# Attention and MLP on one core: the key corners written by a maximum or on ScalarE, the identity loaded first, and a new written order of all tasks

## The chip, the core and the metric

The kernel runs on one core of one Trainium2 chip. The metric is the device time of one execution in microseconds (us). The core has five engines that run side by side: TensorE (PE in the profile; its weight loads stand under PEld), VectorE (DVE), ScalarE (ACT), GpSimd (POOL) and SyncE (SP). Each engine works through its own list of instructions in order, and waits at an instruction whose inputs are not there yet. TensorE writes into PSUM, which has eight banks here, and transfers run on DMA queues that SP, ACT and POOL fill.

## What is computed

An attention with a relative bias over 8 batches, 8 heads, 576 positions and a head size of 64, followed by an MLP with a sine over all 4608 tokens:

```python
scores = scale * np.matmul(q, k.transpose(0, 1, 3, 2)) + bias      # bias depends on |i - j| alone
attn = np.exp(scores - max); attn = attn / (np.sum(attn) + 1e-09)
x = np.matmul(attn, v)                                              # heads side by side: 4608 x 512
h = x @ w_in                                                        # 512 -> 2048
s = np.sin(alpha * h)
g = h + s * s / (alpha + 1e-09)
return g @ w_out                                                    # 2048 -> 512
```

## The kernel before

The work is a graph of 1791 tasks (`_graph`, line 46). Each task has a key, the engines that it may run on, what it emits and what it depends on. The string `ORDER` (line 313) lists the keys in one sequence that was written in advance; `_planned` reads it, and each engine gets its instructions in exactly this sequence. A word is a key, with the PSUM bank behind a slash for TensorE's tasks, and with a letter there (A for ACT, D for DVE, G for POOL) where a task leaves its usual engine. Nothing is rescheduled at run time.

The keys that matter here, with t the batch 0 to 7, p the pair of heads 0 to 3, w the half of the queries and h the half of the keys:

- `n`, `t`, `c`: for t below 3, a load of q or k by POOL's queue (L550), its transposes on TensorE (L654, L670) and the copy out of PSUM by DVE or ACT (L619, L617). For t of 3 and more, `g` stages q or k in DRAM as fp16 on POOL's queue (L577) and `k` reads it back transposed on SP's queue (L583).
- `T`, `X`, `S`: the score tiles. `T` (L727) is four matmuls on 64 rows of the array each; `X` and `S` (L714, L687, L692) do the 64 positions that are left of 576 after four blocks of 128. `E` with the key behind it is the exponential on ACT (L734, L701), `B` with the key is the product with the bias on DVE (L755, L739, L742, L707).
- `o`: the key corners (L589). For t of 2 and more, the last 64 keys of a pair of heads are put on the diagonal of the tile `kd`, by two DVE copies of 64 partitions by 256 elements, SBUF to SBUF; `X` and `S` of the same t read `kd`.
- `A` and `N`: probabilities times v (L769, L778) and the division (L788, L789). `Y` brings the result transposed into `xT`, by SP's queue (L795) for t of 1 and more.
- `I`, `Z`, `Q`, `G`: the MLP's first product (L812), the sine on ACT (L818), its square on DVE (L825) or ACT (L823), and g on DVE (L830), for nine blocks of 512 tokens. `O`, `W`, `D` are the second product (L840), its eviction on DVE or ACT and the store.
- At the start: `r` are the four first loads of q and k, `f` their casts (L617, L619), `id` the load of the identity matrix that every transpose reads (L521), `j` the loads of the bias bands (`toep`, L628) and `m` the four masks that are cut out of them (two copies each, L634).

v is loaded by POOL's queue (`v` L556, `y` L562), as are the weights (L567, L572).

Of the kernel before, what the change touches and what calls it, by code (L numbers as in the profile page):

```python
# [318 lines left out]
EX00 n120 BT0111 X03/4 m0 ET0010 S0/7 BT0000 T0311/2 t101/6 BX00 ES0 BT0001 ET0311 c101 A000/7 m2
BX01 EX03 T0300/0 n131 BT0011 A010/6 BT0010 ET0300 BT0110 T0301/2 N000 m3 X02/4 N010 ET0301  # L320
T0201/0 n201 BS0 t100/7 BT0300 A011/6 v10 EX02 c100 y11 T0210/2 ET0201 BX03 T0310/4 N011 A001/7
n211 ET0210 BT0301 BT0311 n210 A030/6 ET0310 N001 v12 T0200/0 T1000/2 N030 t121/7 ET0200 n231
t111/5 BT0310 c121 t120/6 y10 t130/4 ET1000 T0211/0 BT0201 t131/7 c120 n200 ET0211 T1001/2 c111
A031/6 n230 ET1001 c130 wi3 t221/5 N031 T1110/0 c131/A v13 X10/2 c221/A BX02 T1111/6 BT0200 wi2
P03/4 EX10 BT0211 A020/5 wi1 ET1110 Y03 P01/3 BT0210 P00/2 A021/4 ET1111 N020 Y01 T1011/0 y20 N021
T1100/6 ET1011 t201/5 v11 t231/3 Y00 P02/4 c201 ET1100 X11/0 v23 Y02 S1/5 t200/2 c231 EX11 t210/4
wo0 T1101/6 BT1100 I0.14/3 ES1 wo2 ET1101 c210 wo1 T1010/0 BT1011 X12/4 ET1010 c200 I0.12/7 BT1001
EX12 BT1111 I0.1/6 v22 BX11 Z0.12 BS1 t230/2 BT1000 t211/5 I0.8/4 BT1010 c211 BX10 I0.3/1 Z0.14
BT1110 Q0.12 n220 Q0.14/A BT1101 I0.7/5 G0.12 v20 Z0.3 G0.14 I0.10/0 Z0.1 wo3 Q0.3 Z0.7 A110/7
Q0.1 g41 G0.3 Z0.8 I0.5/3 Q0.7/A G0.1 I0.13/1 c230/A G0.7 Q0.8/A I0.9/6 N110 v21 Z0.10 G0.8 I0.0/7  # L330
Z0.5 Q0.10 Z0.13 Q0.5 A100/2 G0.10 Q0.13/A I0.2/5 Z0.9 G0.5 y21 I0.4/4 Q0.9/A G0.13 Z0.2 N100
A101/3 Z0.4 G0.9 Z0.0 I0.6/2 Q0.4 g31 Q0.2/A G0.4 I0.11/6 Q0.0/A G0.2 Z0.6 I0.15/4 N101 Z0.11
T1300/0 Q0.6 Z0.15 A111/5 G0.0 ET1300 G0.6 O0.0/7 O0.2 Q0.11 Q0.15 T1210/2 O0.4 G0.15 O0.6 ET1210
G0.11 T1200/0 O0.8 BX12 ET1200 N111 T1201/2 t220/6 ET1201 T1211/4 Y11 c220 X13/0 O0.10 ET1211
BT1200 O0.12 o2 T1301/2 EX13 BT1211 T1310/4 O0.14 BT1201 ET1301 A120/6 W0 T1311/0 ET1310 BT1210 D0
X20/2 N120 O1.0/7 BT1301 ET1311 BT1300 S2/6 A121/5 Y10 BX13 EX20 O1.2 N121 T2001/0 ES2 T2011/2
BX20 ET2001 Y12 T2000/4 BT1311 O1.4 BT1310 A130/6 ET2000 O1.6 N130 ET2011 T2010/0 X22/4 A131/6
ET2010 T2211/2 EX22 N131 v31 T2100/0 O1.8 BT2010 Y13 ET2211 O1.10 BT2011 g40 O1.12 BT2000 O1.14
ET2100 BT2001 T2201/2 BS2 T2111/4 W1 ET2201 X21/0 v30 D1 A200/7 ET2111 BT2201 A201/6 g50 N200 EX21
T2210/2 N201 T2101/4 I1.1/7 ET2210 g30 T2110/0 ET2101 BT2210 T2200/2 BT2111 I1.13/6 ET2200 BT2100  # L340
I1.0/5 BT2101 BX22 ET2110 v32 BT2211 I1.4/4 BX21 Z1.13 BT2200 y31 I1.11/3 BT2110 y30 I1.6/2 v33
Z1.4 Q1.13 O2.0/1 Z1.0 G1.13 I1.3/0 Z1.1 Q1.4 O2.2 Q1.0 Q1.1/A I1.9/6 G1.4 Z1.11 G1.0 I1.12/4 Z1.3
G1.1 Q1.11/A I1.5/5 Q1.3 Z1.12 G1.11 I1.2/7 Z1.6 Q1.12 Q1.6/A G1.3 I1.14/3 Z1.5 G1.6 I1.15/0 Z1.2
G1.12 Q1.2/A I1.8/2 Q1.5 Z1.15 G1.2 I1.7/4 Z1.9 G1.5 Q1.9/A I1.10/7 Q1.15 Z1.7 G1.15 k30 A220/5
Q1.7/A G1.9 A221/0 Z1.8 N220 Z1.14 A210/6 G1.7 Z1.10 O2.4 N221 Q1.10/A T2311/4 k31 O2.6 Q1.8
ET2311 N210 A211/0 G1.10 O2.8 N211 O2.10 T2300/6 Q1.14 Y20 X23/4 G1.8 ET2300 O5.0/0 G1.14 O5.2
EX23 T2310/6 Y22 T2301/2 O2.12 ET2310 O2.14 T3000/4 ET2301 k40 T3001/6 BT2310 BT2300 O5.4 ET3001
O5.6 o3 O5.8 W2 O5.10 ET3000 BX23 T3010/2 BT2311 X30/6 ET3010 Y21 BT2301 S3/1 O5.12 BT3000 X31/4
ES3 EX30 O5.14 A230/1 W5 EX31 T3100/2 N230 T3110/6 D5 A231/0 ET3100 BT3001 BX31 D2 BS3 BX30
T3101/4 ET3110 v40 BT3100 T3211/2 A300/1 BT3010 ET3211 N231 g51 O4.0/7 O4.2 N300 Y23 ET3101 O3.0/6  # L350
BT3211 T3210/0 T3011/2 o4 T3111/4 ET3210 O4.4 g70 BT3101 O4.6 ET3011 O4.8 O4.10 ET3111 BT3011
T3201/0 X32/2 g61 ET3201 O4.12 A301/5 EX32 A310/4 N301 v41 T3200/0 X33/2 BT3201 Y30 N310 ET3200
I2.1/5 v42 BT3111 EX33 I2.10/4 BX32 y41 k41 Z2.1 y40 O4.14 I2.9/3 g60 I2.15/2 W4/A Q2.1 I2.5/1
Z2.10 BT3200 Z2.9 I2.14/7 Q2.10 G2.1 Q2.9/A A320/0 G2.10 Z2.14 I2.7/5 G2.9 Z2.15 Q2.15/A I2.3/4
N320 v43 Z2.7 Q2.14 I2.13/3 G2.15 Z2.3 G2.14 Q2.3/A I2.8/2 Z2.13 G2.3 I2.0/7 Z2.8 BT3210 Q2.7
I2.11/4 Q2.13/A G2.7 Q2.8/A I2.6/0 G2.13 Z2.11 G2.8 I2.4/5 Z2.5 Q2.11 Q2.5/A I2.2/3 G2.11 Z2.0
BT3110 O3.2 Z2.4 G2.5 I2.12/4 Z2.2 Q2.0 Q2.4/A G2.0 O3.4 S4/2 Q2.2/A O3.6 G2.4 A321/7 Z2.12 Z2.6
Q2.12 O3.8 BX33 ES4 A311/5 G2.2 Q2.6 O3.10 G2.6 O3.12 T3310/2 G2.12 T4001/0 O3.14 ET3310 N321
O7.0/4 ET4001 W3 O7.2 T3301/2 N311 T3311/6 O7.4 ET3301 Y31 O7.6 ET3311 T4000/0 T3300/2 O7.8 ET3300
D3 O6.0/5 O7.10 ET4000 k51 T4010/6 BT3300 X40/2 O6.2 ET4010 BT4000 O7.12 BT3310 T4100/0 EX40  # L360
BT4010 X41/6 BS4 BT4001 O6.4 BT3301 ET4100 BT3311 Y32 O6.6 A330/3 EX41 A331/2 N330 D4 T4011/0 N331
v53 T4210/6 O7.14 ET4011 BX40 O6.8 Y33 v51 W7 ET4210 T4101/2 T4211/0 BT4011 g71 O6.10 k50 ET4101
BT4100 A400/4 O6.12 ET4211 N400 T4111/2 T4200/6 BT4101 A401/4 BX41 y50 ET4111 v52 O6.14 ET4200
N401 T4201/0 y51 X42/2 W6 ET4201 I3.10/4 v50 BT4210 BT4211 EX42 T4110/6 BT4111 X43/0 A410/5 ET4110
I3.6/3 EX43 BT4110 BT4201 T4310/6 BX42 A411/2 BT4200 ET4310 N410 I3.3/1 Z3.6 I3.15/5 A420/0 Z3.3
Q3.6 I3.0/7 N411 Z3.10 I3.2/6 G3.6 Z3.0 Q3.3 Q3.0/A I3.12/2 G3.3 I3.1/3 N420 Z3.12 G3.0 Q3.10/A
I3.7/1 Z3.15 G3.10 I3.14/7 Q3.12/A Z3.2 I3.5/4 G3.12 Q3.15/A BX43 O8.0/0 Q3.2 Z3.7 A421/2 G3.15
Z3.14 G3.2 I3.8/5 Q3.7/A N421 Z3.5 I3.9/6 Z3.1 G3.7 Y42 I3.13/2 Q3.14/A o5 Z3.9 G3.14 I3.11/1 D7
Q3.5/A Y40 I3.4/7 Q3.9/A G3.5 Z3.13 Q3.1 O8.2 Z3.4 G3.9 O8.4 O9.0/4 Q3.13/A G3.1 O9.2 Q3.4/A G3.13
O8.6 Z3.8 O9.4 G3.4 O8.8 Z3.11 Q3.8 T4300/2 T4301/6 G3.8 O9.6 ET4300 BT4310 O8.10 Q3.11 O10.0/5  # L370
G3.11 O8.12 O8.14 ET4301 S5/1 O9.8 W8 O10.2 ES5 T4311/2 D8 T5001/6 T5000/0 ET4311 O10.4 k60 O9.10
ET5001 BT4311 O10.6 O9.12 BT4301 ET5000 BT4300 T5010/2 X50/6 ET5010 A430/1 BT5000 D6 O10.8 EX50
# [533 lines left out]
```

## Time and profile before

| | us |
|---|---|
| three runs | 389.81, 392.21, 392.63 |
| median of them | 392.21 |
| the profiled execution | 388.54 |
| its span, from first to last instruction | 386.6 |
| PE, ACT, DVE busy in the span | 371.4, 313.2, 271.3 |

The page shows one execution. Matmuls are pipelined, so a busy PE is not a PE that does useful work in every cycle; what it loses is better read from the times between the starts of its matmuls, and from the waits that the trace names. The clock that was granted to TensorE is 1.0 in every stage.

### The profile page before, as it was taken

What the parts mean: (1) busy time and instruction counts of PE and PEld (TensorE: products, weight loads), DVE (VectorE), ACT (ScalarE), POOL (GpSimd) and SP (SyncE); (2) the same over time, 40 slices, a digit from 0 to 9 for tenths busy, and PEclk for the clock granted to TensorE, in tenths of its full rate; (3) what the DMA queues carried; (4) which work ended last, traced back from release to release, by engine and by line L of the source; (5) the groups of instructions that cost most, each with busy time, mean ns of one, the idle gap of its engine ahead of it and who ended that gap; (6) DMA issues with size and microseconds to landing.
All of it is one profiled execution on the core that took longest, in us unless ns stands there. A gap on an engine that the chain in (4) does not pass through costs nothing.

```text
span 386.6 us, 9237 instructions
## 1 busy us (share of the span) xinstructions
PE 371.4 (96%) x3811; PEld 204.1 (53%) x3811; DVE 271.3 (70%) x625; ACT 313.2 (81%) x422; POOL 83.9 (22%) x100
## 2 busy tenths in 40 slices
PE   4999999999997999899999999999999999999996
PEld 3577455645554456554664544556555444444453
DVE  4599999679796977497668958685476577852311
ACT  5999999999996999899999999999895578654101
POOL 7878550470066004300000080000000000000000
PEclk9999999999999999999999999999999999999999
DMA  9999999999999969932938096031412011000115
GB/s 161 197 200 170 196 193 154 93 164 169 158 119 157 158 45 168 151 21 63 197 31 199 17 176 48 2 63 47 91 46 63 0 54 56 0 1 28 43 67 190
DMA packets 142617, 40.14 MB, mean 104 GB/s; under 512 B 127552, under 2 KB 138096, under 8 KB 142576
## 3 DMA queue, kind: packets, MB, share of 16 engines
q0 software_dynamic: 92672, 18.06, 57.0%
q1 hardware_dynamic: 47904, 18.94, 24.4%
q10 hardware_dynamic: 2000, 2.56, 1.9%
q8 instruction: 29, 0.48, 0.5%
q14 instruction: 12, 0.10, 0.1%
HBM read 36.89 MB, written 15.34 MB: 135 GB/s over the span
## 4 chain that ended last, share of the span: by engine, by line
PE 74%; DMA 9%; ACT 6%; DVE 5%; POOL 3%; issue 2%; SPq 0%; POOLq 0%; ACTq 0%
PE acc L840 29%; PE acc L812 26%; PE acc L778 7%; PE acc L727 6%; DMA w_in<-in_moe_w_in_dram 3%; ACT u L734 3%; DMA toep<-e_sb 2%; DMA xT<-xp 2%; PE acc L687 2%; PE acc L769 2%; ACT s L818 2%; DMA xT<-in_k_dram 2%; DVE g L830 1%; DVE kd L589 1%; POOL xT L550 1%
## 5 line engine op out<-in xcount | busy, mean ns | idle before, releaser
L734 ACT ACTIVATE u<-acc 128x1024 f16<-128x1024 f32 x160 | 152.0, 1035 | 13.4 <-PE acc L727 11.0
L840 PE MATMUL acc<-w_out,g 128*128 128x512 f16 (+1 forms) x592 | 141.8, 374 | 0.0
L812 PE MATMUL acc<-xT,w_in 128*128 128x512 f16 x576 | 135.0, 379 | 2.0 <-DMA xT<-xp 1.2
L830 DVE SCALAR_TENSOR_TENSOR g<-s,inv_a,acc 128x512 f16<-128x512 f16 x144 | 103.2, 744 | 17.3 <-ACT s L823 11.6
L818 ACT ACTIVATE s<-acc,alphaT 128x512 f16<-128x512 f32 x144 | 92.4, 686 | 25.9 <-PE acc L812 24.4
L812 PEld LDWEIGHTS <-w_in 128*128 128x128 f16 x576 | 54.6, 98 | 64.9 <-DMA w_in<-in_moe_w_in_dram 1.7
L840 PEld LDWEIGHTS <-g 128*128 128x128 f16 x592 | 54.0, 98 | 56.7 <-issue 5.5
L755 DVE TENSOR_TENSOR u<-u,toep 128x256 f16<-128x256 f16 (+1 forms) x128 | 58.9, 488 | 22.4 <-ACT u L734 21.3
L556 POOL DMA_DIRECT2D v<-in_v_dram x32 | 33.9, 1117 | 129.0 <-PE acc L778 125.6
L778 PE MATMUL acc<-v,u 128*128 128x65 f16 x1280 | 54.1, 193 | 2.7 <-DVE u L755 2.7
L778 PEld LDWEIGHTS <-u 128*128 128x128 f16 x1280 | 49.9, 97 | 7.2 <-DVE u L755 2.9
L825 DVE TENSOR_TENSOR s<-s 128x512 f16<-128x512 f16 x77 | 32.0, 421 | 19.5 <-ACT s L818 19.3
L727 PE MATMUL acc<-qT,kT 64*128 64x256 f16 x512 | 43.5, 281 | 0.5 <-ACT qT L617 0.5
L823 ACT ACTIVATE s<-s 128x512 f16<-128x512 f16 x67 | 41.1, 629 | 0.9
L727 PEld LDWEIGHTS <-kT 64*128 64x128 f16 x512 | 19.2, 96 | 28.0 <-issue 24.5
L789 DVE TENSOR_TENSOR xp<-acc,rden 128x256 f16<-128x256 f32 (+1 forms) x64 | 31.4, 491 | 2.2
L617 ACT ACTIVATE outs<-acc 128x512 f32<-128x512 f32 (+1 forms) x16 | 9.3, 582 | 25.3 <-PE acc L840 25.3
L619 DVE COPY outs<-acc 128x512 f32<-128x512 f32 (+1 forms) x21 | 13.9, 676 | 22.5 <-PE acc L840 22.4
L769 PE MATMUL acc<-vt,u 128*128 128x130 f16 x128 | 28.2, 220 | 0.1
L788 DVE RECIPROCAL rden<-acc 128x4 f32<-128x4 f32 (+1 forms) x64 | 11.8, 185 | 14.5 <-PE acc L778 12.1
L769 PEld LDWEIGHTS <-u 128*128 128x128 f16 x128 | 12.4, 97 | 6.3 <-issue 2.3
L562 POOL DMA_DIRECT2D vt<-in_v_dram x16 | 14.4, 906 | 5.7 <-issue 2.1
(60 smaller groups left out, 195.7 us busy)
## 6 DMA issues: line engine op xcount, KB each, us to landing
out_dram<-outs SPq DMA_DIRECT2D x28, 256.0 KB, 2.3
v<-in_v_dram POOLq DMA_DIRECT2D x32, 128.0 KB, 6.9
staged_q<-in_q_dram POOLq DMA_DIRECT2D x5, 576.0 KB, 14.0
staged_k<-in_k_dram POOLq DMA_DIRECT2D x5, 576.0 KB, 11.9
w_in<-in_moe_w_in_dram POOLq DMA_DIRECT2D x4, 512.0 KB, 10.1
w_out<-in_moe_w_out_dram POOLq DMA_DIRECT2D x4, 512.0 KB, 13.2
out_dram<-outs ACTq DMA_DIRECT2D x7, 256.0 KB, 2.1
xT<-in_q_dram POOLq DMA_DIRECT2D x11, 144.0 KB, 5.7
```

The source lines that it names most:

```text
L556: self.nc.gpsimd.dma_start(out=self.vs[t % 2][:, c, :, 0:D], in_=src)
L727: self.nc.tensor.matmul(out=s[:, o:o + 256], lhsT=self.kT[t % 2][r, p, 128 * c:128 * c + 128], rhs=self.qT[t % 2][r, p, 256 * w:256 * w + ...
L734: self.nc.scalar.activation(out=c["u"], in_=c["s"], func=AF.Exp, scale=0.125)
L755: self.nc.vector.tensor_tensor(out=io, in0=io, in1=m, op=ALU.mult)
L769: nc.tensor.matmul(out=c["av"][:, 130 * j:130 * j + 130], lhsT=tail, rhs=vt[:, p, :], start=True, stop=True, skip_group_check=True)
L778: nc.tensor.matmul(out=c["av"][:, 130 * j + 65 * a:130 * j + 65 * a + 65], lhsT=l, rhs=vv[:, ch, 2 * p + a, 0:65], start=False, stop=True, ...
L812: self.nc.tensor.matmul(out=c["h"], lhsT=self.w_in[:, j, 128 * f:128 * f + 128], rhs=self.xT[:, j, 512 * b:512 * b + 512], start=(j == 0), ...
L818: self.nc.scalar.activation(out=c["s"], in_=c["h"], func=AF.Sin, scale=self.alphaT[:, f:f + 1])
L823: self.nc.scalar.activation(out=c["s"], in_=c["s"], func=AF.Square)
L825: self.nc.vector.tensor_tensor(out=c["s"], in0=c["s"], in1=c["s"], op=ALU.mult)
L830: self.nc.vector.scalar_tensor_tensor(out=self.g[b][:, f, :], in0=c["s"], scalar=self.inv_a[:, f:f + 1], in1=c["h"], op0=ALU.mult, op1=ALU ...
L840: self.nc.tensor.matmul(out=c["mo"], lhsT=self.g[b][:, f, 128 * (tau % 4):128 * (tau % 4) + 128], rhs=self.w_out[:, f, at], start=(f == 0) ...
```

## The change

The corners take another instruction. On DVE it is a maximum of the source with itself, which gives the source; on ACT it is a copy:

```diff
-    def corners(self, t):
+    def corners(self, t, act):
         kT, kd = self.kT[t % 2], self.kd[t % 2]
         for a in range(2):
             r = slice(64 * a, 64 * a + 64)
-            self.nc.vector.tensor_copy(out=kd[r, :, 64 * a:64 * a + 64],
-                                       in_=kT[r, :, 512:576])
+            dst, src = kd[r, :, 64 * a:64 * a + 64], kT[r, :, 512:576]
+            if act:
+                self.copy(dst, src, True)
+            else:
+                self.nc.vector.tensor_tensor(out=dst, in0=src, in1=src, op=ALU.max)
```

The task may now run on either engine (`add(f"o{t}", "DVE ACT", ...)`). Lines below 592 move down by three.

The whole of `ORDER` is replaced. The graph is the same, so each engine's tasks are the same but for those that may choose. The new order puts `o4` and `o6` on ACT and the other four corners on DVE; five more of the `c` copies go to ACT (6 to 11), `f00` and `f11` to DVE, the masks `m0` and `m3` from POOL to DVE, the bands `j2` and `j3` from SP's queue to POOL's; six squares fewer are done by ACT (67 to 61), one eviction more. Its beginning:

```diff
-r10/A r00 ms id/A r01 n011 r11/A sub n010 cst tab al n030 n031 f00/A f10 th00/7 n110 th10/6 ch00
-n020 ch10/A f01/A T0000/0 v01 th01/7 ET0000 v03 t011/6 bu/5 f11/A y01 c011 t010/4 be n021 th11/3
-bs ch01 c010/A bm/6 y00 T0001/0 ch11/A bc v02 T0100/2 ET0001 j1 T0101/4 n101 T0011/6 ET0101 X01/0
+id/A r00 ms r10/A r01 n010 r11/A sub n011 cst tab al n120 n021 f00 n100 th00/7 f10 n030 ch00
+th10/6 f01/A n020 ch10/A th01/7 y01 T0000/0 ch01/A bu/7 ET0000 f11 T0001/2 t010/6 be n031 ET0001
+bs th11/7 y00 bm/5 ch11 t011/4 c010 bc v00 T0011/0 c011/A j0 T0010/2 v03 ET0011 T0100/4 X00/6 v02
+ET0100 j1 t021/1 j2/G ET0010 t100/0 c021 T0101/4 EX00 v01 T0111/2 ET0101 j3/G X01/6 BT0011 ET0111
+t020/1 n110 BT0000 T0110/4 EX01 n111 m0/D c100 at/3 c020/A t030/2 m1 av ET0110 t120/7 BT0101 n210
```

Four places farther on, new order only: the score tiles of batch 1, the corners of batch 3, those of batch 4, and the last words.

```
T1301/2 X20/4 BT1310 BT2001 ET1301 A120/7 BT1210 BT1300 A121/1 EX20 N120 T2011/2 t211/7
...
EX21 T2301/2 T2101/0 BT2100 O1.6 ET2101 BT2211 A220/6 Y13 v31 BX21 T2110/4 ET2301 N220 X23/0 v33 O1.8
BT2101 ET2110 A221/6 o3 v32 EX23 A210/5 ... T3011/4 BT2111 T3001/2
...
O5.4 O4.12 G1.14 o4/A T3201/2 D1 T3310/4 T3200/0 ET3201 O5.6 O5.8 ET3200
...
O31.10 O31.12 W30 D35b O31.14 O35.4a D30 W31/A O35.8a O35.12a D31 W35a/A D35a/A
```

Counted in TensorE's sequence, `T` tiles stood alone 38 times, in twos 34 times, in threes 6 times and in a four once; now it is 31, 32 and 11 times.

More of the change, by code (lines that the diff above doesn't have):

```diff
@@ L149, in _graph @@
                     turn(t, p, kind, old_qk)
-            corner[t] = add(f"o{t}", "DVE", lambda e, b, t=t: K.corners(t),
+            corner[t] = add(f"o{t}", "DVE ACT", lambda e, b, t=t: K.corners(t, e == "ACT"),
                             [kT[t, p][0] for p in range(NP)] + [ms])
@@ L159, in _graph @@
                 if not kind:
-                    corner[t] = add(f"o{t}", "DVE", lambda e, b, t=t: K.corners(t), [c, ms])
+                    corner[t] = add(f"o{t}", "DVE ACT", lambda e, b, t=t: K.corners(t, e == "ACT"), [c, ms])
         v_in[t] = [add(f"v{t}{c}", "POOL", lambda e, b, a=(t, c): K.load_v(*a), [ms, *old_av])
@@ L319 @@
[L319 to L372, printed above, removed]
@@ L427 @@
-W35a/A D35a/A
+id/A r00 ms r10/A r01 n010 r11/A sub n011 cst tab al n120 n021 f00 n100 th00/7 f10 n030 ch00
[3 more added lines that the diff above has]
+t020/1 n110 BT0000 T0110/4 EX01 n111 m0/D c100 at/3 c020/A t030/2 m1 av ET0110 t120/7 BT0101 n210
@@ new lines @@
+BT1010 Q0.7 Q0.4/A v21 G0.9 I0.12/2 Z0.14 G0.4 g31 Z0.1 t200/6 G0.7 t221/5 c200/A I0.10/1 Q0.14
+Z0.12 Q0.1 G0.14 A100/6 Z0.15 g30 I0.11/3 G0.1 c221/A Z0.10 BX11 T2000/4 Q0.15 O0.0/7 Z0.11 N100
+O0.2 Q0.10/A G0.15 A101/6 ET2000 Q0.12 G0.10 O0.4 O0.6 G0.12 T1211/0 Q0.11 O0.8 N101 ET1211 A110/2
+G0.11 T1200/4 T1201/0 N110 A111/6 ET1200 ET1201 T2001/2 N111 T1300/4 O0.10 ET2001 BT2000 O0.12 Y11
+O2.0/6 o2 ET1300 T1210/0 BT1211 T1310/2 O2.2 BT1200 ET1310 Y10 O0.14 BT1201 O2.4 ET1210 W0 T1301/2
+X20/4 BT1310 BT2001 ET1301 A120/7 BT1210 BT1300 A121/1 EX20 N120 T2011/2 t211/7 BX20 ET2011 X13/4
@@ new lines @@
+N121 A200/0 BT1301 EX13 c211 T1311/2 O2.6 N200 ET1311 k31 T2010/4 BX13 T2210/0 A130/7 ET2010
+BT1311 S2/3 O2.8 N130 ES2 T2200/4 ET2210 BT2011 T2201/2 A131/7 D0 BT2010 ET2201 O2.10 N131 y31
+ET2200 Y12 T2211/0 X22/2 y30 BS2 BT2201 O1.0/7 BT2210 EX22 g61 A201/5 k30 ET2211 T2100/2 N201
+O2.12 ET2100 O1.2 BX22 BT2200 v30 T2300/0 X21/4 ET2300 Y20 O2.14 g40 O1.4 W2 EX21 T2301/2 T2101/0
+BT2100 O1.6 ET2101 BT2211 A220/6 Y13 v31 BX21 T2110/4 ET2301 N220 X23/0 v33 O1.8 BT2101 ET2110
+A221/6 o3 v32 EX23 A210/5 N221 g50 T2111/2 T2311/0 BT2301 Y22 O1.10 N210 ET2311 O3.0/6 BX23 O3.2
@@ new lines @@
+BT2300 ET2111 O3.4 g41 BT2110 T2310/0 T3011/4 BT2111 T3001/2 ET2310 O1.12 BT2311 O3.6 ET3011
+A211/1 ET3001 T3101/4 N211 A230/0 ET3101 O3.8 N230 T3000/2 T3111/4 BT3101 ET3000 BT2310 X30/0
+O3.10 O1.14 EX30 O3.12 W1 T3110/2 ET3111 X31/0 O3.14 ET3110 A231/7 W3 EX31 T3100/4 N231 v42
+T3010/2 I1.11/6 ET3010 BT3111 Y23 v41 S3/7 BX30 I1.1/1 ET3100 BX31 v40 BT3011 T3210/2 ES3 BT3001
+X32/4 Y21 ET3210 BS3 I1.7/7 BT3100 BT3000 EX32 I1.2/0 BT3010 k40 Z1.1 A300/3 A310/2 N300 I1.8/5
+Z1.11 Q1.1 I1.3/4 G1.1 I1.6/3 Q1.11 Z1.3 N310 Z1.7 I1.4/1 Q1.3 Q1.7/A G1.11 I1.9/2 Z1.2 G1.7 Z1.4
@@ new lines @@
+I1.0/6 G1.3 Q1.4/A Q1.2 I1.5/7 Z1.8 G1.2 Z1.6 I1.15/4 BT3110 Q1.8 Z1.5 G1.4 I1.13/0 Q1.6/A G1.8
+Z1.0 I1.10/1 G1.6 Z1.9 I1.12/5 Q1.5 Z1.13 Q1.0 G1.5 Q1.13/A A301/3 Q1.9/A G1.0 A311/7 Z1.12 G1.13
+Z1.10 O5.0/6 G1.9 O5.2 N311 I1.14/0 Z1.15 N301 Q1.15/A O4.0/7 k41 Z1.14 O4.2 Q1.10 Q1.12 T3300/2
+G1.10 O4.4 ET3300 O4.6 Q1.14 G1.12 O4.8 O4.10 G1.15 D2 O5.4 O4.12 G1.14 o4/A T3201/2 D1 T3310/4
+T3200/0 ET3201 O5.6 O5.8 ET3200 BT3201 O4.14 O5.10 W4 ET3310 T3211/0 X33/2 BT3300 D4 ET3211 O6.0/7
+BT3210 O6.2 Y30 X40/4 EX33 BT3211 S4/1 O6.4 ES4 O5.12 BX33 EX40 BT3200 O6.6 T3311/0 BX32 T4001/2
@@ new lines @@
+Q5.10/A I5.11/7 G5.5 G5.7 O23.0/4 Z5.11 O23.2 BT6310 G5.10 Z5.9 A631/6 Z5.12 Q5.9 O19.2 Q5.11/A
+G5.9 X70/2 G5.11 O23.4 EX70 A621/0 Q5.12 N631 O19.4 G5.12 O23.6 O23.8 N621 T7001/6 T7010/2 Y62
+T7011/0 ET7001 O19.6 O19.8 ET7011 BT7001 O19.10 D17 O19.12 ET7010 Y63 T7101/0 T7000/6 O19.14
+ET7101 O23.10 Y61 W19 T7100/2 ET7000 X71/0 O23.12 D16 ET7100 O21.0/5 BT7000 O21.2 BX70 EX71
+T7110/6 BT7011 T7211/2 O23.14 ET7110 BX71 A700/1 BT7010 BT7100 O21.4 W23/A O21.6 N700 ET7211
+T7201/6 X72/0 O21.8 EX72 A701/4 ET7201 O21.10 N701 T7200/0 T7111/2 BT7101 X73/6 ET7200 Y70 BT7211
@@ L428 @@
+O35.8a O35.12a D31 W35a/A D35a/A
 """
```

134 lines of the change are left out of this document (78 added, 56 removed).

## Prediction

> **What bounds the kernel now.** I read the page first, then the stretches (second fence: start and end, length, then busy time of PE, PEld, DVE, ACT and POOL), then what TensorE waited for (third: in total, times, longest).
>
> ```profile
> span 386.6 us, 9237 instructions
> PE 371.4 (96%) x3811; PEld 204.1 (53%) x3811; DVE 271.3 (70%) x625; ACT 313.2 (81%) x422; POOL 83.9 (22%) x100
> ```
> ```profile
> 0.00:20.00 20.00, 13.62 (x197) 9.11 (x197) 10.57 (x31) 14.26 (x20) 16.39 (x29) 1.00 1.29 181
> 20.00:70.00 50.00, 48.75 (x799) 30.93 (x798) 47.40 (x121) 48.71 (x64) 25.80 (x33) 1.00 1.60 181
> ```
> ```profile
> PE acc L654 <- DMA ident<-eye: 4.9, 1, 4.9
> PE acc L778 <- DVE u L755: 2.7, 1, 2.7
> PE acc L812 <- DMA xT<-xp: 1.2, 1, 1.2
> ```
>
> TensorE is the bound from 20 us on. ACT and DVE are as full as TensorE between 20 and 70 us (48.71 and 47.40 of 50). TensorE's work is the same before and after, matmul for matmul; an order can win only what TensorE loses. The third fence lists that: 4.9 us at the start, then 2.7 and 1.2, and nothing else above 1 us.
>
> The largest loss has its cause on DVE:
>
> ```profile
> L589 DVE COPY kd<-kT x12: 210/224/5244, 63.7 to 218.3; 64x256 f16<-64x256 f16 x12
> ```
> ```profile
> 111.91 5.48 DVE L589 COPY kd<-kT 64x256 f16<-64x256 f16 x2
> ```
> ```profile
> 110.28 2.23 POOL L577 DMA_DIRECT2D staged_q<-in_q_dram  x1
> ...
> 117.13 2.23 POOL L562 DMA_DIRECT2D vt<-in_v_dram  x1
> ```
> ```profile
> 118.38 0.35 PE L778 MATMUL acc<-v,u 128*128 128x65 f16 x6 [2.73 <-DVE u L755]
> ```
>
> One of the twelve corner copies (`o4`) took 5.24 us, where the median is 0.22. POOL issued transfers all that time, from 110.28 to past 117.13. The band products behind the copy came late, and `A301` stood 2.73 us in its middle. This is execution, not a wait for the keys: the other copy of the pair reads the same transposed keys and had finished.
>
> **The corners.** As a maximum, the four DVE corners become 8 products of two SBUF operands, 64x256. Prices nearby:
>
> ```profile
> L734 ACT ACTIVATE u<-acc 128x1024 f16<-128x1024 f32 x160 | 152.0, 1035 | 13.4 <-PE acc L727 11.0 <-PE acc L687 0.7 <-ACT u L734 0.5
> ...
> L823 ACT ACTIVATE s<-s 128x512 f16<-128x512 f16 x67 | 41.1, 629 | 0.9
> ...
> L755 DVE TENSOR_TENSOR u<-u,toep 128x256 f16<-128x256 f16 x64 | 17.9, 287 | 8.1 <-ACT u L734 8.0
> ```
>
> 8 x 0.287 = 2.3 us against 8 x 0.224 = 1.8 us: 0.5 us more on DVE, which has the time after 70 us. Every L755 product has two SBUF operands, and none of the 64 of this shape can have been held by 5 us, since their mean is 0.287; I take the hold as gone. Bounds: 2.73 us won, or nothing if the maximum is held too. On ACT, 4 copies of 64x256 cost less than L823's 0.63 each, which has twice the elements: at most 2.5 us, on an engine that after 70 us has them to spare. They add a wait in ACT's queue: behind `o4/A` stands `ET3201`, and the score banks wait for it. The cover:
>
> ```profile
> 101.49 2.25 SPq L583 DMA_TRANSPOSE kT<-staged_k  x1
> ```
> ```profile
> kT<-staged_k SPq DMA_TRANSPOSE x5, 6.1
> ```
>
> On SP's queue `k40` stands right behind `Y23` and `Y21`, and between `A231`, which feeds `Y23`, and `T3201`, next to `o4`, TensorE has 16 `I` and 10 `O`: at 0.86 us for four such matmuls (fence below) 13.8 + 4.3 = 18 us, where the read takes 2.25 us to issue and 6.1 to land. Cost 0; without that cover ACT would stand for the rest of the landing, and TensorE soon after.
>
> **The order: switches of the array.** From the chain of waits:
>
> ```profile
> 58.63 0.86 PE acc L840 x4
> 59.82 0.97 PE acc L840 x4
> ...
> 179.40 0.54 PE acc L727 x8
> ...
> 183.19 0.76 PE acc L727 x12
> ```
>
> Four full matmuls take 0.86 us, or 0.97 when score tiles follow; four more score matmuls cost 0.22, so eight should take 0.44 and take 0.54 up to the next full one. A change between full and 64-row matmuls costs 0.1 us. Counted in TensorE's list, there are 137 such changes before and 131 after: 6 x 0.1 = 0.6 us won. Three score tiles in a row are rarer than the words say (11 places), so this part is small.
>
> **The order: `xT` for block 2.** The old order has 20 tasks of TensorE between `A231` and `I2.1`; the read of `Y23` took 7.32 us (chain: DMA xT<-xp) and TensorE waited 1.2.
>
> ```profile
> 151.08 7.32 DMA xT<-xp
> ```
>
> The new one has 74 tasks there, 16 `I` and 27 `O` among them: 13.8 + 11.6 = 25 us at least, so 1.2 us are won. The reverse is `k31` and `k30`, closer to their use than before: 37 tasks with 14 `O`, 13 `T`, 6 `A`, 3 `X` and an `S` stand between `T1311`, which frees their tile, and `T3011`; `O` and `T` alone are 6.0 + 3.5 us, with the `A` some 14. Two reads of 2.25 us to issue, the second 6.1 to land, make 10.6 us, with a store and `Y12` between. I take 0, with 0 to 3 us to lose.
>
> **The start.**
>
> ```profile
> 1.19 0.48 ACTq L521 DMA_DIRECT2D ident<-eye  x1
> ...
> 3.93 1.34 POOL L550 DMA_DIRECT2D xT<-in_k_dram  x2
> 3.98 0.52 ACT L617 ACTIVATE xT<-toep 96x384 f16<-96x384 f32 x1
> 4.15 0.36 DVE L619 CAST xT<-toep 96x384 f16<-96x384 f32 x1 [0.69 <-DMA toep<-in_q_dram]
> 4.86 0.61 PE L654 MATMUL acc<-ident,xT 96*64 96x96 f16 x10 [4.86 <-DMA ident<-eye]
> ```
>
> Both casts ended at 4.50 and 4.51; the transposes stood until 4.86 for the identity. Issued first, it is 0.46 us earlier, but q's first half is then 0.46 later and its cast with it, some 0.1 us behind the old place of the second transpose. `f00` on DVE no longer waits for ACT's table. Between 0 and 0.36 won; I take 0.3.
>
> **The other moves.**
>
> ```profile
> 10.43 5.49 SPq L628 DMA_DIRECT2D toep<-e_sb  x8
> ```
> ```profile
> L634 POOL COPY mt<-toep 64x192 f16<-64x192 f16 x8 | 3.0, 371 | 2.7 <-DMA toep<-e_sb 2.5
> ...
> L619 DVE COPY qT<-acc 128x576 f16<-128x576 f16 x9 | 6.8, 750 | 2.1 <-PE acc L670 2.1
> ```
>
> The bands `j2` and `j3` are four of eight transfers, 0.69 us each on SP, so 2.7 us move to POOL's queue, ahead of `v01`, `n110` and all weights, which come that much later; four mask copies of 0.37 and half of the 2.7 us that POOL waited for them leave it, 2.8 us. Even: 0. On DVE those four copies cost some 0.22 each, as a corner did, between 16 and 23 us; five `c` of 0.75 leave DVE and more than pay. ACT gets the five at about L823's 0.63, and gives 6 squares of 0.63 and two of its 16 table loads, since the order goes 14 times between exponential and sine. After 70 us neither engine is on the path: 0. A hold of the masks is a rival below.
>
> What I do charge is ACT's lead. Up to `A120` in the old order ACT has 35 large exponentials, 16 sines and 7 squares behind it, and that was just enough:
>
> ```profile
> 64.13 0.89 DVE L755 TENSOR_TENSOR u<-u,toep 128x1024 f16<-128x1024 f16 x2
> ```
> ```profile
> 65.01 0.22 PE L769 MATMUL acc<-vt,u 128*128 128x130 f16 x1
> ```
>
> The band ended at 65.02 and `A120` started at 65.01. Up to `A121` the new order asks for 39, 16 and 5, five `c` more and two casts fewer: 4 x 1.035 + 5 x 0.63 - 2 x 0.63 - 2 x 0.52 = 5.0 us more of ACT, for only 2.4 us more of TensorE (three `O` at 0.43, two `T` at 0.27, an `A` estimated at 0.6). The 2.6 us must come from ACT's idle time: 5.7 us of the first 20 (20 - 14.26) and 1.3 of the next 50. The new start lets the second exponential go before `t010` and not after `t011`, `t010` and the rest, and later each score tile stands farther ahead of its exponential. I take 0.6 us as lost, between 0 and 2.6.
>
> **Sum:** -2.7 - 1.2 - 0.6 - 0.3 + 0.6 = -4.2 us on the profiled execution (388.54, span 386.6). That execution is 3.7 us below the median of the runs, a gap that I carry over unexplained: 392.2 - 4.2 = 388.0.
>
> **Rivals.** *The lead is short:* the whole 2.6 us are waited, 390.0. For it: the zero margin at `A120`; against it: the 7 us that ACT has to give.
>
> *The masks are held:* `m0` and `m3` on DVE meet POOL's loads of q, k and v as `o4` met its stagings. Two holds of 5.0 us (5.24 - 0.22) less the 2.6 us that DVE has free between 20 and 70 us put 7.4 us on TensorE: 388.0 + 7.4 = 395.4, slower than before; it decides from 6.8 us of holds on (4.2 + 2.6). Against it: the cast at 4.15 us, SBUF to SBUF on DVE, took 0.36 us in the middle of two issues of POOL (3.93 to 5.27), and the first copy of `o4` was not held. The Trainium skill, "SBUF — State Buffer", section "Who interferes with whom", speaks for it: copies and casts on DVE can take the port pair shared with GpSimd, and the second to come "fully blocks" until the first is done, while a product of two SBUF inputs collides only with a GpSimd instruction that reads SBUF. The hold of `o4` agrees with it, the cast at 4.15 us does not.
>
> *The form of the corner doesn't matter:* something else held SBUF at 112 us and holds the maximum too. The 2.7 us stay: 390.7. Nothing in the trace excludes it; that no two-operand product was ever held speaks against it.
>
> *More was lost than one execution shows:* the 3.7 us between this execution and the median are further holds of corners in the other runs, and go too: 384.3.
>
> **Numbers.** The forecast 0.48 (by itself 385.5 to 390), short lead 0.20, masks held 0.12, form doesn't matter 0.10, more lost 0.10. A measurement of this kernel tells about 1% from no change, 388.3 to 396.1. Faster by over 1%: six in ten of the forecast (0.29), a quarter of the short lead (0.05), nearly all of the last (0.09) and 0.02 of the form: 0.45. Slower by over 1%: half of the held masks (0.06: a third or fourth hold of 5 us), and 0.06 of the forecast and the short lead, for waits on transfers that no row of before can bound: 0.12. The rest, 0.43, is the same. The range 384.5 to 394.5 leaves out half of the last rival, the worse half of the masks and those 0.06.
>
> **What would show it.** Right: `kd` written by products of some 0.29 us, none above 0.5, and no wait of TensorE for L755 above 0.5 us; no wait for xT<-xp; first transpose at 4.5 to 4.6 us. Wrong: a mask copy of microseconds on DVE with POOL issuing; TensorE waiting for DVE or ACT around 65 us; a wait of `T30` or `X30` for kT or qT<-staged around 85 us; a corner on ACT behind which exponentials start late. The forecast falls above all if the time of TensorE's first 70 us, which I count as unchanged, grows.

## The result, and the profile after

The changed kernel takes 385.77 us in the median of four runs (385.26 to 386.24), the kernel before 391.95 (389.81 to 392.63) beside it: the ratio is 0.985, 95% interval 0.981 to 0.989. It is faster by 1.5%. The forecast was 4.2 us less, the medians differ by 6.2, and the two profiled executions by 3.3 (388.54 and 385.26). One run among those of the experiments, 392.40 us of `before_o4_late`, lies in the chip's slower state and counts neither in its median nor in its ratio. So there are two questions: why the traces show less than the forecast, and why the medians show more.

The page of the changed kernel, its span, its engines and TensorE's granted clock in 40 slices:

```profile
span 383.4 us, 9217 instructions
PE 371.0 (97%) x3811; PEld 205.8 (54%) x3811; DVE 264.2 (69%) x627; ACT 313.0 (82%) x422; POOL 84.5 (22%) x100
...
PEclk9889999999999999999999999999999999999999
```

The trace records TensorE's clock only from its first change on, at 18.0 us in the profiled execution of the kernel before and at 11.96 us here. Ahead of that a view shows 1.0 without a record behind it, so "1.0 in every stage" does not hold for the start: in the kernel before, eight score products took 1.03 us at 14.66 us and 0.61 us at 25.12 us.

The account of the 3.2 us in the span comes from the stretches. Columns: start and end, length, busy time of PE, PEld, DVE, ACT and POOL, the granted clock, and the share and rate of the transfers. First the three stretches of the kernel before that the prediction did not show, then all five of the changed one:

```profile
70.00:130.00 60.00, 57.03 (x639) 32.11 (x636) 48.07 (x108) 55.69 (x72) 25.13 (x19) 1.00 1.60 144
130.00:200.00 70.00, 68.81 (x780) 38.73 (x779) 52.41 (x125) 64.74 (x86) 7.92 (x8) 1.00 0.91 105
200.00:386.60 186.60, 183.19 (x1408) 93.21 (x1406) 112.89 (x242) 129.83 (x184) 8.67 (x11) 1.00 0.32 62
```
```profile
0.00:20.00 20.00, 13.11 (x199) 8.88 (x199) 9.54 (x34) 14.58 (x20) 14.62 (x27) 0.88 1.26 181
20.00:70.00 50.00, 48.82 (x771) 31.13 (x766) 45.80 (x117) 48.16 (x63) 28.22 (x36) 0.98 1.54 172
70.00:130.00 60.00, 60.00 (x761) 35.18 (x758) 44.85 (x117) 56.77 (x72) 16.24 (x13) 1.00 1.45 143
130.00:200.00 70.00, 70.00 (x654) 37.30 (x651) 48.63 (x114) 63.79 (x86) 19.38 (x17) 1.00 1.24 123
200.00:383.40 183.40, 179.11 (x1447) 93.32 (x1444) 115.40 (x248) 129.70 (x185) 6.01 (x8) 1.00 0.28 59
```

Length less PE's busy time is what TensorE stood idle. Before and after:

| stretch | idle before | idle after | difference |
|---|---|---|---|
| 0 to 70 us | 7.63 | 8.07 | +0.44 |
| 70 to 130 us | 2.97 | 0.00 | -2.97 |
| 130 to 200 us | 1.19 | 0.00 | -1.19 |
| 200 us to the end | 3.41 | 4.29 | +0.88 |
| PE busy in all | 371.40 | 371.05 | -0.35 |
| span | 386.60 | 383.40 | -3.20 |

The two waits that the prediction named are gone: TensorE has no idle time left between 70 and 200 us. The last stretch, which it did not treat, gives 0.9 back. The waits of TensorE that are left (in total, times, longest) lie before 60 us:

```profile
PE acc L657 <- DVE xT L622: 4.4, 2, 3.8
PE acc L598 <- DMA tab<-in_bias_table_dram: 1.2, 1, 1.2
...
PE acc L673 <- DMA xT<-in_k_dram: 0.2, 1, 0.2
```

The corners on DVE are eight products, none of them held (minimum, median and maximum in ns):

```profile
L593 DVE TENSOR_TENSOR kd<-kT x8: 276/284/290, 64.6 to 239.4; 64x256 f16<-64x256 f16 x8
```

The start of the changed kernel, in order of time:

```profile
3.41 0.36 DVE L622 CAST xT<-toep 96x384 f16<-96x384 f32 x1
...
3.82 0.45 PE L657 MATMUL acc<-ident,xT 96*64 96x96 f16 x6 [3.82 <-DVE xT L622]
...
4.81 0.81 PE L657 MATMUL acc<-ident,xT 96*64 96x96 f16 x12 [0.54 <-DVE xT L622]
...
7.63 0.56 PE L598 MATMUL acc<-tab,sub 32*128 32x8 f32 x2 [1.25 <-DMA tab<-in_bias_table_dram]
```

The first transposes come 1.04 us earlier (3.82 against 4.86), but the second ones wait for q, and the product of the bias waits for its table.

### The profile page after: what moved, and what is told of

Same layout as the page of the kernel before. It is cut to its first block, busy times and chain, and to the rows that moved or that the text cites. A ratio compares the mean times of both kernels' runs of the same rounds, so it can differ in the third digit from the quotient of the medians.

```text
span 383.4 us, 9217 instructions
## 1 busy us (share of the span) xinstructions
PE 371.0 (97%) x3811; PEld 205.8 (54%) x3811; DVE 264.2 (69%) x627; ACT 313.0 (82%) x422; POOL 84.5 (22%) x100
## 4 chain that ended last, share of the span: by engine, by line
PE 90%; DMA 5%; POOL 1%; issue 1%; ACT 1%; SPq 1%; DVE 0%; ACTq 0%; POOLq 0%; DVEq 0%
PE acc L843 33%; PE acc L815 32%; PE acc L781 9%; PE acc L730 8%; PE acc L772 2%; PE acc L690 2%; DMA xT<-in_k_dram 2%; DMA toep<-e_sb 2%; DMA tab<-in_bias_table_dram 1%; PE acc L673 1%; PE acc L717 1%; DMA out_dram<-outs 1%; POOL xT L550 1%; POOL mt L637 0%; PE acc L695 0%
## 5 line engine op out<-in xcount | busy, mean ns | idle before, releaser
L737 ACT ACTIVATE u<-acc 128x1024 f16<-128x1024 f32 x160 | 153.7, 1031 | 15.2 <-PE acc L730 13.8
L758 DVE TENSOR_TENSOR u<-u,toep 128x256 f16<-128x256 f16 (+1 forms) x128 | 58.6, 486 | 21.3 <-ACT u L737 18.6
L556 POOL DMA_DIRECT2D v<-in_v_dram x32 | 31.4, 1083 | 110.0 <-PE acc L781 73.3
L828 DVE TENSOR_TENSOR s<-s 128x512 f16<-128x512 f16 x83 | 33.9, 418 | 18.2 <-ACT s L821 18.1
L826 ACT ACTIVATE s<-s 128x512 f16<-128x512 f16 x61 | 37.3, 631 | 1.4 <-ACT outs L620 0.4
L562 POOL DMA_DIRECT2D vt<-in_v_dram x16 | 11.9, 752 | 18.2 <-PE acc L781 17.6
```

The costliest lines, as they stand in the source:

```text
L556: self.nc.gpsimd.dma_start(out=self.vs[t % 2][:, c, :, 0:D], in_=src)
L737: self.nc.scalar.activation(out=c["u"], in_=c["s"], func=AF.Exp, scale=0.125)
L758: self.nc.vector.tensor_tensor(out=io, in0=io, in1=m, op=ALU.mult)
L826: self.nc.scalar.activation(out=c["s"], in_=c["s"], func=AF.Square)
L828: self.nc.vector.tensor_tensor(out=c["s"], in0=c["s"], in1=c["s"], op=ALU.mult)
```

## The experiments

Each kernel was timed six times, before_again twelve times. Each ratio is to the kernel before, run in turn with it on the same chip; its median there was 390.91, 391.38 and 391.18 us in the three groups of timed kernels.

| kernel | median us | ratio, 95% interval |
|---|---|---|
| before_again | 391.08 | 0.999, 0.996 to 1.003 |
| before_max | 386.82 | 0.988, 0.985 to 0.992 |
| before_o4_late | 385.69 | 0.986, 0.982 to 0.991 |
| before_g_early | 397.18 | 1.017, 1.012 to 1.022 |
| after_again | 385.59 | 0.985, 0.981 to 0.988 |
| after_copy | 384.95 | 0.983, 0.980 to 0.987 |
| after_late_id | 385.16 | 0.984, 0.980 to 0.988 |
| after_tab | 387.23 | 0.989, 0.986 to 0.993 |
| after_tail | 384.88 | 0.984, 0.980 to 0.989 |
| after_bands | 385.83 | 0.987, 0.982 to 0.991 |
| after_best | 384.03 | 0.983, 0.979 to 0.987 |

The theory was the prediction's: the hold of one plain copy is the largest loss of the kernel before, and the two-operand form removes it. Its rivals: the form doesn't matter; more was lost than one execution shows. The experiments added a third: the new place of the corners is enough.

### The corners

**before_max**, the form alone:

```diff
-            self.nc.vector.tensor_copy(out=kd[r, :, 64 * a:64 * a + 64],
-                                       in_=kT[r, :, 512:576])
+            dst, src = kd[r, :, 64 * a:64 * a + 64], kT[r, :, 512:576]
+            self.nc.vector.tensor_tensor(out=dst, in0=src, in1=src, op=ALU.max)
```

> The kernel before with the corners as a maximum of two operands and nothing else changed. My theory: the hold of o4 goes, all twelve products take 0.28 to 0.30 us, the wait of 2.73 us at A301 goes, 2.7 us less on a comparable execution (ratio near 0.993, some 389.2 us against 391.95). If the form doesn't matter, one of the products takes over 1 us while POOL issues transfers and the time is the same (ratio 1.000). If more was lost than one execution shows, the ratio is 0.985 to 0.99 and with it most of the change's 6.2 us.

**before_o4_late**, the place alone; the copies stay plain:

```diff
-T3210/0 T3011/2 o4 T3111/4
+T3210/0 T3011/2 T3111/4
...
-BT3110 O3.2 Z2.4
+BT3110 o4 O3.2 Z2.4
```

> The kernel before with nothing changed but the place of o4 in the order: its plain copies stand behind the exponential and band of T3110, where DVE is at some 135 us and POOL issues nothing (127 to 150 us), and not at 112 us between POOL's issues. If the hold is a meeting of a plain copy with POOL's issues, both copies take 0.22 us, A301 does not wait, and the time falls as with the maximum: 2.7 to 4.1 us less, ratio 0.988 to 0.993. If the first of the two copies waits for its keys, or if plain copies are held whatever POOL does, one still takes microseconds at 135 us and bands behind it come late; the ratio stays at 0.998 to 1.000.

Each of the two edits alone takes 1.2 to 1.4% off, more than the theory's 2.7 us. Beside each other on one chip, before_o4_late takes 385.69 us and the whole change (after_again, below) 385.59: moving one word of the old order earns as much as all of the change, within the intervals. The corners of before_max, and of before_o4_late:

```profile
L590 DVE TENSOR_TENSOR kd<-kT x12: 276/284/290, 64.7 to 216.3; 64x256 f16<-64x256 f16 x12
```
```profile
L589 DVE COPY kd<-kT x12: 208/218/224, 64.4 to 216.3; 64x256 f16<-64x256 f16 x12
```

The same 107 products around `A301`, in the kernel before, in before_max and in before_o4_late (each stretch runs from the start of the 1501st product to that of the 1601st):

```profile
114.55:126.41 11.86, 9.13 (x107) 5.48 (x104) 8.12 (x17) 8.24 (x11) 8.47 (x8) 1.00 2.31 155
```
```profile
115.65:124.60 8.95, 8.95 (x107) 5.43 (x104) 4.60 (x14) 8.23 (x11) 5.41 (x6) 1.00 2.29 157
```
```profile
115.40:124.35 8.95, 8.95 (x107) 5.43 (x104) 4.59 (x14) 8.23 (x11) 5.40 (x6) 1.00 2.28 156
```

11.86 us become 8.95 in both: 2.9 us, by the form or by the place. So the hold was neither a wait for the keys nor a matter of plain copies as such; it is a plain copy at that moment, amid POOL's issues. That POOL is the other party is read from the times, and no run takes POOL's issues away and leaves the rest as it was: in all three traced executions of the kernel before, the held copy ends 0.03 us after POOL begins to issue the load of v at L562 (117.13 us in the prediction's row), and its twin then takes 0.22 us although POOL is still issuing. That the form doesn't matter is refuted for the old order.

**after_copy**, the form undone in the new order:

```diff
-                self.nc.vector.tensor_tensor(out=dst, in0=src, in1=src, op=ALU.max)
+                self.nc.vector.tensor_copy(out=dst, in_=src)
```

> The changed kernel with its four corners on DVE as plain copies again (o4 and o6 stay on ScalarE). In its trace POOL issues transfers from 81.3 to 85.0 us and o3 is at 83.6; o2, o5 and o7 lie where POOL issues nothing. My theory: a copy of o3 is held until POOL pauses, at most 1.4 us (85.0 less 83.6), the others take 0.22; the time is 385.8 to 387.2, since the new order has kept the corners out of POOL's way. If the form is what the change gains by, the time rises by 2.7 us or more, to 388.5 and above. If POOL's issues have nothing to do with it, no copy is held and the time stays at 385.8.

It is no slower. Only the pair of `o3` falls among POOL's issues. Its first copy took 0.54 us, the other 0.22, and the first was free again 0.8 us before POOL paused, so it was not, as had been expected, held until the burst ended:

```profile
L593 DVE COPY kd<-kT x2: 224/382/539, 82.4 to 83.0; 64x256 f16<-64x256 f16 x2
```
```profile
80.10 3.68 POOL L556 DMA_DIRECT2D v<-in_v_dram  x3
```

In the changed kernel the maximum therefore earns nothing that can be measured: of its four corners on DVE three lie where POOL issues nothing, and `o3` costs 0.3 us more as a copy. What plain copies of `o4` and `o6` would cost on DVE in the new order was not run.

**before_g_early**, to learn which issues of POOL hold a copy:

```diff
-T3101/4 ET3110 v40
+T3101/4 ET3110 g51 g70 g61 v40
...
-N231 g51 O4.0/7
+N231 O4.0/7
...
-O4.4 g70 BT3101
+O4.4 BT3101
...
-X32/2 g61 ET3201
+X32/2 ET3201
```

> The kernel before, the corners plain copies at their old place, but POOL's three stagings of k and q (g51, g70, g61) stand ahead of the load v40 in its queue and not behind it, so that they issue at some 86 us, and at 112 us POOL issues only loads of v. If it is the stagings that hold the copy, o4 takes 0.2 to 0.6 us, as o3 did among loads of v with the plain copies in the new order (0.54), A301 does not wait, and the ratio is 0.985 to 0.99. If any issue of POOL holds it until the burst ends, o4 takes 1 to 4 us and the ratio is 0.99 to 0.997. If POOL is not the cause, o4 takes 5.2 us again, the ratio is 1.000.

The copies did as the first case says, 0.32 us at loads of v (the first met only the last 0.3 us of one); the time did not:

```profile
L589 DVE COPY kd<-kT x2: 224/270/317, 127.7 to 128.0; 64x256 f16<-64x256 f16 x2
```
```profile
125.31 2.67 POOL L556 DMA_DIRECT2D v<-in_v_dram  x3 [24.38 <-PE acc L778]
```
```profile
PE acc L727 <- DMA qT<-staged_q: 9.5, 1, 9.5
```
```profile
96.27 5.51 SPq L583 DMA_TRANSPOSE kT<-staged_k  x1
101.88 8.10 SPq L583 DMA_TRANSPOSE qT<-staged_q  x1
```

The stagings now run while SP reads q and k back transposed; those reads take 5.5 and 8.1 us to issue where the prediction's row has 2.25, and TensorE waits 9.5 us. In the kernel before, the two reads that run beside stagings took 6.4 and 5.7 us (from 121.5 and 152.4 us), the others 2.1 to 3.7. The kernel ends 1.7% slower, with a wait for transfers that the corner has no part in (the traced execution, 400.94 us, is the slowest of the six, 3.8 above their median). So stagings are under suspicion, but this run is no clean proof: in the kernel before, the copy was also held while POOL issued loads of v behind the stagings.

### Why the medians show more than the traces

**before_again** and **before_third** are the kernel before, unchanged.

> The kernel before, unchanged, to see what the 3.7 us between its profiled execution (388.54) and the median of its runs are. If they are further holds of corner copies, this execution shows kd copies of microseconds, in another number or at another length than the one of 5.24 us, and its time goes with them. If they are the opening of TensorE's clock, which the changed kernel's trace shows at half speed from 15.4 to 22.2 us, then the executions above 390 have a mean granted clock below 1.00 and the holds stay as they were. If neither, TensorE's stalls are spread differently. Expected time 389.8 to 392.6 in any case.

> A third traced execution of the kernel before. The first two took 11.86 and 13.43 us for the same 107 products around A301; the second had TensorE's clock at half speed from 120.2 to 123.6 us, right behind the hold. If the hold itself is constant, o4 takes 5.2 us a third time; if the clock behind it is what spreads the times of this kernel, the stretch takes 11.9 us with the clock open and 13.4 us or more with it closed, and nothing between.

The third took 390.88 us, in one run. The hold is constant: 5.24 us in all three traced executions, and in each it is the first copy of the pair that is held. In the first of them:

```profile
L589 DVE COPY kd<-kT x1: 5244/5244/5244, 111.9 to 111.9; 64x256 f16<-64x256 f16 x1
```

What spreads is, for one, what follows it. The same stretch of products took 11.86 us there, and in before_again and before_third (a product at the edge is counted in the latter):

```profile
114.93:128.36 13.43, 10.71 (x107) 6.04 (x104) 9.39 (x18) 8.56 (x12) 8.48 (x8) 0.87 2.27 157
```
```profile
115.95:129.15 13.20, 10.48 (x108) 6.69 (x104) 8.19 (x17) 8.24 (x11) 8.49 (x8) 0.87 2.31 157
```

The granted clock is 0.87 in both (13.20 us is a little less than was expected with the clock closed). In windows of 3.41 us, laid on the moments at which the trace records a change of the clock, around the wait of 2.7 us; first the execution of the prediction, then before_again, then before_third:

```profile
113.58:116.99 3.41, 2.07 (x23) 1.07 (x21) 3.41 (x1) 3.21 (x4) 3.41 (x4) 1.00 2.08 128
116.99:120.40 3.41, 2.02 (x55) 1.90 (x56) 2.22 (x8) 0.05 (x1) 2.97 (x4) 1.00 2.46 156
120.40:123.82 3.42, 3.42 (x18) 1.63 (x18) 1.41 (x6) 3.39 (x4) 0.47 (x2) 1.00 2.46 157
```
```profile
113.35:116.76 3.41, 2.68 (x26) 1.32 (x24) 3.41 (x1) 3.41 (x5) 3.41 (x4) 1.00 2.15 126
116.76:120.18 3.42, 1.43 (x42) 1.43 (x42) 2.22 (x6) 0.41 (x1) 2.96 (x4) 1.00 2.41 156
120.18:123.59 3.41, 3.41 (x24) 1.65 (x21) 2.00 (x7) 2.63 (x3) 0.62 (x1) 0.50 2.46 157
```
```profile
116.02:119.43 3.41, 1.03 (x17) 0.60 (x11) 3.37 (x4) 2.18 (x3) 3.41 (x5) 1.00 2.39 155
119.43:122.84 3.41, 3.07 (x48) 2.85 (x50) 1.53 (x6) 0.00 (x0) 1.93 (x3) 0.50 2.46 158
```

Where the wait fell across two windows (2.07 and 2.02 us busy), the clock stayed. Where it left one window with 1.43 or 1.03 us busy, the next ran at half clock. The Trainium skill, "TensorE: Matmul & The Clock Gate", section "Part 1: The HAM clock gate (the "warmup" mystery)", describes a gate that judges free-running windows of 4096 cycles, 3413 ns; the length and the shifting phase agree with these traces, while its "after ≥1 idle window" does not cover them, since here windows that were 30 and 42% busy were followed by half clock. The busy time alone does not decide it either: in the changed kernel the window from 11.96 us, with 2.28 us busy, was followed by half clock, and in after_late_id the one from 28.48 us, with 1.70 us, was not.

So the hold costs 2.9 us, and 4.2 to 4.5 (13.20 - 8.95 and 13.43 - 8.95) where the clock closes behind it. The form alone won 4.1 us between the medians. The prediction's execution was a lucky one: of 53 later timed executions of the kernel before, one alone is shorter (388.39).

The clock behind the hold is a part of the "3.7 us carried over unexplained", and not all of it. The two later executions exceed the first by 2.4 and 2.3 us. They lost 1.6 and 1.3 us in the stretch above, and got back some at the wait for `xT`, which fell from 1.2 to 0.4 and 0.8 us. Ahead of the hold they were already 0.4 and 1.4 us behind (start of the 1501st product); in before_third the first record of full clock is at 23.86 us and not at 18.0. In before_again 1.3 us more lie outside the span (3.2 us between time and span, where most executions have 1.9). What sets the median of 391 to 392 us is not shown beyond this, and the granted clock does not sort the times: two executions at 0.981 have spans of 388.2 and 392.1 us.

### The start and the early stretch

**after_late_id**:

```diff
-id/A r00 ms r10/A r01 n010
+r10/A r00 ms id/A r01 n010
```

> The changed kernel with the identity issued behind q's first half, as before. My theory: the first transposes go back from 3.8 to 4.9 us, but the wait of 1.2 us for the bias table at 7.6 us takes that up, so that by 10 us TensorE is as far as in the changed kernel; the time stays within 0.3 us of 385.8. If the start carries through, the time rises by 1.0 us, to 386.8. If the early start is what closes the clock again at 15.4 us, the half-speed stretch goes and the time falls by 1 us or more, to 384.8.

**after_tab**:

```diff
-id/A r00 ms r10/A r01 n010 r11/A sub n011 cst tab al
+id/A r00 ms r10/A sub tab r01 n010 r11/A n011 cst al
```

> The changed kernel with the matrix and the table of the bias issued ahead of the second half of k on SP's queue. In the changed kernel the table lands at 7.5 us and TensorE waits 1.2 us for it. If that wait is a loss, the product of the bias starts at 6.4 to 6.9 us, the bands' table and the masks come 0.7 to 1.0 us earlier, and the end with them: 384.8 to 385.1 us. If the second half of k, now 0.9 us later, takes its place, or the stretch up to 40 us is set by POOL's loads, the time is the same within 0.3 us.

The identity's place is worth nothing in the time (385.16 against 385.59 to 385.77): the first transposes are 1.0 us later without the edit (4.84), and by the 51st product, at 9.54 us, TensorE is as far as in after_again (9.43). And the table cannot be had for nothing. Issued ahead of the second half of k, it makes that half the wait, at a higher price than foreseen, and the kernel 1.6 us slower than after_again; the start of after_tab:

```profile
3.89 0.99 PE L657 MATMUL acc<-ident,xT 96*64 96x96 f16 x12 [3.89 <-DVE xT L622]
8.26 0.45 PE L657 MATMUL acc<-ident,xT 96*64 96x96 f16 x6 [3.38 <-ACT xT L620]
```

**after_bands**:

```diff
-j2/G
+j2
...
-j3/G
+j3
...
-m0/D
+m0
...
-m3/D
+m3
```

> The changed kernel with the bands j2 and j3 issued by SP again and the masks m0 and m3 copied by POOL again, in the same places of the order. The forecast counted this move as even. If so, the time stays within 0.5 us of 385.6. If the move had a price, by POOL's loads of the first tiles coming later, the time falls to 384.5 or below. If it had a gain, by masks that no longer stand between POOL's loads, the time rises to 386.6 or above.

385.83 against 385.59: even, as forecast.

**after_again**, the base of these:

> The changed kernel, unchanged, as the base for the three beside it. Expected 385.0 to 386.3 us and a ratio of 0.983 to 0.989. If its early stretch differs from execution to execution as the kernel before's does, the stretch at half clock lies elsewhere than 15.4 to 22.2 us this time, and the start of the 700th product moves by up to 1 us with it.

Its clock was at half speed from 19.0 to 25.9 us where the first trace had 15.4 to 22.2, and its 701st product starts at 51.90 us and not at 51.03. In after_late_id the clock never closed again. A start moved by 1 us lies inside this spread, and no run here separates the two causes.

### The end

**after_tail**:

```diff
-        o = self.tp.tile([128, DM], F32, name="outs", tag="outs", bufs=3)
+        o = self.tp.tile([128, DM], F32, name="outs", tag="outs", bufs=4)
```

> The changed kernel with four buffers for the output tiles where it has three. In its trace the last eviction but one stands on ScalarE until a store has landed (3.65 us idle, released by a store, at 378.96), and the last quarter's eviction behind it: from the last product's start to the end of the span 4.56 us, where the kernel before has 3.62. If that is a loss that the sum lacked, the last stretch falls to 3.6 to 4.0 us and the time by 0.6 to 0.9 us. If the stores are bound by the transfer itself, the last stretch stays at 4.3 to 4.6 us and the time too.

The last work of ScalarE and the last store's issue, in the kernel before, the changed kernel, and after_tail:

```profile
383.29 0.38 ACT L617 ACTIVATE outs<-acc 128x256 f32<-128x256 f32 x1 [0.23 <-PE acc L840]
383.70 0.34 ACTq L853 DMA_DIRECT2D out_dram<-outs  x1
```
```profile
378.96 0.87 ACT L620 ACTIVATE outs<-acc 128x512 f32<-128x512 f32 x2 [3.65 <-DMA out_dram<-outs]
379.87 0.35 ACTq L856 DMA_DIRECT2D out_dram<-outs  x1
```
```profile
379.19 1.01 ACT L620 ACTIVATE outs<-acc 128x512 f32<-128x512 f32 x2 [3.30 <-DMA out_dram<-outs]
380.23 0.34 ACTq L856 DMA_DIRECT2D out_dram<-outs  x1
```

In the new order a whole eviction, which waits for a buffer, stands on ACT ahead of the last quarter's. From the start of the last product to the end of the span it takes 4.6 to 4.8 us in all the traces of the new order with three buffers, and 3.9 in after_tail, near the 3.6 of before (382.98 to 386.6). A part is the eviction (the last product to the issue of the store: 0.72 before, 1.03 after, 0.77 in after_tail), the rest the landing of the store behind the others. Four buffers do not end the wait for a store, which is still 3.30 us of idle time there. Nor is the old order free of it: in before_max one store took 3.8 us to land where the other traces of that order have 2.0, ACT waited for it, and the end took 4.8 us; that is one of six traces of the old order, against all six of the new one with three buffers. The 0.9 us are shown in the trace; in the times the medians differ by 0.7, and the intervals do not tell them apart.

**after_best** adds to that the place of one load:

```diff
-A010/7 wi2 BT0010
+A010/7 BT0010
...
-BX02 n231
-t111/0
+BX02 n231
+wi2 t111/0
```

> The changed kernel with four output buffers, and with the load of the third quarter of w_in (wi2) moved in POOL's queue from ahead of n220 to behind n231. In three of five traces of the changed order TensorE stood 0.3 to 2.7 us in front of t220 at 31 to 33 us, for n220, which lands behind that load of 512 KB. If that wait is a loss that stays, the time falls by 0.3 to 1.5 us beside the 0.7 of the buffers: 383.4 to 384.6 us. If the load is then late for I0.8, or the next transposes wait in place of t220, the time stays at 384.9.

The transposes `t220` of after_tail stood behind that load; in after_best they start at 30.78 us and do not wait, and the last product's start to the end takes 3.7 us:

```profile
32.72 0.45 PE L673 MATMUL acc<-ident,xT 96*64 96x96 f16 x12 [2.51 <-DMA xT<-in_k_dram]
```
```profile
30.78 0.45 PE L673 MATMUL acc<-ident,xT 96*64 96x96 f16 x12
```

With 384.03 us it has the lowest median of all, 1.6 below after_again, but the intervals of the two ratios overlap.

## Why the prediction was right, and where not

**The hold.** Right: it was the largest loss, and it went, with no wait for L758 (L755 before). The term was too small. Priced from one execution at 2.7 us, it measures 2.9 there and 4.2 to 4.5 in two others, and the form alone wins 4.1 between medians. The rival "more was lost than one execution shows" had the direction, with the wrong mechanism: no further copies are held. TensorE's clock closes behind the one hold, and the profiled execution also had the best start of the three.

**What removes it.** Only half right. The sum credits the form. In the old order the form does it (before_max), but the place does it as well (before_o4_late), and in the new order the form of the four corners on DVE is superfluous (after_copy). Of the rest of the change no net gain is left to measure beside before_o4_late.

**A misread row.** The prediction says that the second copy of `o4` was held and the first had finished, and builds two arguments on that: execution and not a wait for keys, and one against held masks. It was the first, at 111.9 us; the second took 0.22 at 117.2. The view that it used groups both in one row of 5.48 us; taken apart they read 5.24 and 0.22. The first conclusion is borne out otherwise (before_o4_late); the second argument falls. The masks met no issue of a load by POOL in the trace, so that rival was not put to the test.

**The corners on ACT.** Right at 0: no wait of TensorE for them.

**`xT`.** The wait went, 1.19 us as said (0.4 and 0.8 us in before_again and before_third, so it too was sized from one execution), but the place was wrong. TensorE stood in front of `I3.10`, in block 3:

```profile
158.44 0.38 PE L812 MATMUL acc<-xT,w_in 128*128 128x512 f16 x1 [1.20 <-DMA xT<-xp]
```

The read at 151.08 us is `Y33`, not `Y23`, by its place in SP's queue: the four of the first batch go through TensorE and do not stand there. Between `Y33` and `I3` the old order has 11 tasks of TensorE, the new one 58, so the same working gives the same answer.

**The switches of the array.** 0.6 us forecast; PE's busy time fell by 0.35. Stretches at half clock are in that number, so it neither confirms nor refutes 0.1 us a switch, and no run here isolates it.

**The start.** 0.3 us forecast for the first transposes, 1.04 seen, nothing in the time: the wait moved to q's half and to the bias table. The step counted where the first wait ends and not where the next begins.

**ACT's lead.** 0.6 us lost was forecast around 65 us. No wait of TensorE stands there; up to 70 us it lost 0.44 on balance, in the first 60 us. The size was near, the mechanism is not shown: the stretches at half clock fall into the same time.

**The bands and masks.** Even, as counted (after_bands).

**What the sum lacked.** The end: 0.9 us. The order changes which evictions stand ahead of the last one, and the sum stopped at TensorE's last product.

On the two traced executions the terms read -3.0, -1.2, -0.35, +0.4 and +0.9, which makes 3.2 us of span. The forecast of 388.0 lies 2.2 above the median. With the hold at the 4.1 us between medians the terms make 4.3 us of the 6.2 by which the medians differ: its dearer price, less an end that was forgotten. The start of the profiled execution, 0.4 and 1.4 us ahead of the two later ones, is a part of what remains; the rest is open. That the number came within the range is therefore in part luck, since errors of both signs stand in the sum.

## What to carry to other kernels

Before a loss is priced from one profile, see where that execution stands among the runs; one below all of them is a sign that something costs more as a rule. A stall of TensorE is to be priced with the window behind it: some 2.7 us of wait cost 2.9 to 4.5 over the next products. Before a whole order is rewritten, the one task that meets the loss is to be moved alone: here that was worth as much. And the end of a kernel is a step of its own: follow the last eviction and store in the new order, not just the last product.
